# Rounding the gated activations of two chunks in one instruction, with a longer lag to the second product

## The chip, the cores and the metric

One core of one Trainium2 chip runs the kernel. The metric is the device time of one execution in microseconds; a figure for a kernel is the median of several executions.

## The reference, cut to what matters

Three steps run on 8192 tokens of 192 channels in float32: a causal depthwise convolution of seven softmaxed taps, and two feed-forward layers of width 2048, the first with `h * clip(h + 3, 0, 6) / 6` between its two products, the second with ELU.

```python
out = np.einsum('hk,bskhg->bshg', w, x_unf)      # seven taps, softmaxed, per head
...
h = x @ w_in;  g = h * np.clip(h + 3.0, 0.0, 6.0) / 6.0;  x = g @ w_out
...
h = x @ w_in;  g = np.where(h > 0.0, h, np.exp(np.minimum(h, 0.0)) - 1.0);  out = g @ w_out
```

## The kernel before, in words

**Blocks and chunks.** The tokens are cut into 16 blocks of 512 columns; the width of 2048 into 16 chunks of 128. The unit of the order is a chunk of one block of one layer: the list `slots` (L539 to 546) has 512 of them. The text counts layers as the code does: layer 0 (the clipped one) and layer 1 (ELU). Blocks 0 to 5 of layer 0 come first (blocks 0 and 1 interleaved, slots 0 to 31, then 32 to 95), then blocks of layer 1 and of layer 0 alternate, and the last six blocks of layer 1 follow each other.

**Products in two parts.** TensorE takes fp32r operands, so each operand is kept as a rounded part and a rest. `mm1` (L435) makes h of one chunk with five matmuls (four or five of half the contraction in the later stage), `mm2` (L479) adds the chunk into the output sums p with five: the rounded `gh` against three slices of weights, the rest `gl` against two. In the first stage (`stream(ALL, ...)`, slots 0 to `BOTH + LAG - 1`) each matmul uses all 128 rows. After it two streams, the lower and the upper 64 rows of the array, run side by side, the upper one eight matmuls behind; that stage is issued by hand in the order written (`manual_schedule`). A one-element memset of `relay` on POOL (L454) marks the end of each chunk's lower half of h.

**Between the products.** `first_done` (L680) is called when h of slot s is issued. `gate` (L460) makes g from h: one ScalarE activation (two in layer 1: Relu, then Exp in place) into a tile u, and one VectorE `scalar_tensor_tensor` from u and h into a tile g. `split_g` (L472) rounds g into `gh` on ScalarE (CAST) and takes `gl = g - gh` on VectorE; it is called for slot s-1 after the gate of s. h has three PSUM banks, so the first matmul of slot s+3 waits for the gate of slot s. `mm2` of slot s-LAG follows `mm1` of slot s; LAG is 4.

**The planner.** Everything else on VectorE and ScalarE is cut into steps (generators that yield) and put into `jobs` with a first slot a, a last slot e and a count n: decoding the float64 weights, the convolution of later blocks (`conv_main`, `conv_r`), the evaluation of a finished block (`upper_sum`) and the split of layer 0's result (`split_y`). `run_jobs` (L521) runs after each `first_done`; its function `wanted` decides:

```python
if s >= e() - (1 if e() <= BOTH else 2):
    return True
late = done * (e() - a) < n * (s - a + 1)
return late or s < BOTH + LAG and s >= a and debt[0] < 0 and debt[1] < 500
```

So in the later stage a job's steps are spread evenly over its slots, and what is left at the end is run at once. Of several wanted jobs the one with the earliest end goes first.

**Layer 0's result.** `upper_sum` (L367) adds the two halves of a finished block. The rest channels (64 of 192) are kept twice: `yr` of 128 rows is made with two ScalarE copies and one VectorE add; `split_y` (L416) rounds each half on ScalarE and subtracts each half on VectorE.

Of the kernel before, what the change touches and what calls it, by code (L numbers as in the profile page):

```python
# [8 lines left out]
F32 = mybir.dt.float32  # L9
F32R = mybir.dt.float32r  # L10
I32 = mybir.dt.int32
U32 = mybir.dt.uint32
AF = mybir.ActivationFunctionType
ALU = mybir.AluOpType
# [1 line left out]
PSUM = bass.MemoryType.PSUM  # L16

P = 128
LAG = 4
BEHIND = 8  # L20
RA = 6
STAG = 2
# [7 lines left out]
NB = 512  # L30
# [26 lines left out]
def conv_moe_moe2(ctx: ExitStack, tc: tile.TileContext, x, weight, w_in1, w_out1, w_in2, w_out2, out):  # L57
# [28 lines left out]
    LO, UP, ALL = slice(0, R), slice(R, P), slice(0, P)  # L86
    NBLK = NT // NB

    vec, act = Meter(nc.vector, 80), Meter(nc.scalar, 90)
# [3 lines left out]
    xin = ctx.enter_context(tc.tile_pool(name="xin", bufs=2))  # L93
    cv = ctx.enter_context(tc.tile_pool(name="cv", bufs=1))
    tmp = ctx.enter_context(tc.tile_pool(name="tmp", bufs=2))
    gp = ctx.enter_context(tc.tile_pool(name="gp", bufs=LAG + 1))
    yp = ctx.enter_context(tc.tile_pool(name="yp", bufs=RA - 1))
    op = ctx.enter_context(tc.tile_pool(name="op", bufs=3))
    ps_h = ctx.enter_context(tc.tile_pool(name="ps_h", bufs=3, space=PSUM))
# [9 lines left out]
    three = const.tile([P, 1], F32, name="three")  # L109
# [217 lines left out]
    def ring():  # L327


        A = op.tile([P, NB], F32R, name="opA", tag="opA")  # L330
        Bt = op.tile([P, NB], F32R, name="opB", tag="opB")
        lh = op.tile([P, NB], F32R, name="opC", tag="opC")
        hl = op.tile([P, NB], F32R, name="opD", tag="opD")
        return A, Bt, lh, hl
# [17 lines left out]

    spare = {}

    def lower_sum(l, b, lower):

        k = SIXTH if l == 0 else 1.0
        if l == 0:
            y0 = yp.tile([P, NB], F32, name="y0", tag="y0")
        else:  # L360
            y2 = stage.tile([P, 2 * NB], F32, name="y2", tag="raw")
            y0, spare[b] = y2[:, 0:NB], y2[:, NB:2 * NB]
        act.mul(y0, lower[0], k)
        s1 = tmp.tile([P, NB], F32, name="s1", tag="s1", bufs=1)
        act.mul(s1, lower[1], k)
        return y0, s1

    def upper_sum(l, b, upper, y0, s1):


        k = SIXTH if l == 0 else 1.0
        if upper is None:
            yield
        else:
            for i, y in enumerate((y0, s1)):
                vec.scalar_tensor_tensor(out=y, in0=upper[i], scalar=k, in1=y, op0=ALU.mult, op1=ALU.add)
                yield
        if l == 0:
            yr = yp.tile([P, NB], F32, name="yr", tag="yr")
        else:  # L380
            yr = spare.pop(b)
            out0 = store(b, 0, y0)
            next(out0)
        act.copy(yr[LO], s1[UP])
        if l == 0:
            act.copy(yr[UP], s1[LO])
        else:
            yield from out0
        yield
        h = ALL if l == 0 else LO  # L390
        vec.tensor_tensor(out=yr[h], in0=s1[h], in1=yr[h], op=ALU.add)
        yield
        if l == 1:
            yield from store(b, 1, yr)
        else:
            ys[b] = y0, yr

    def store(b, part, y):

        if part == 0:  # L400
            zs[b] = stage.tile([P, 2 * NB], F32, name="z", tag="raw")
        z = zs[b][:, part * NB:(part + 1) * NB]
        h = (ALL, LO)[part]
        vec.transpose(out=z[h], in_=y[h])
        yield
        for k in range(B):
            to = out[k * S + b * HB:k * S + (b + 1) * HB, part * P:part * P + h.stop].rearrange(
                "(j r) d -> r j d", r=SQ)
            for i in range(h.stop // SQ):
                queue = nc.scalar if b == NBLK - 1 and i % 2 else nc.sync  # L410
                queue.dma_start(to[:, :, i * SQ:(i + 1) * SQ],
                                z[i * SQ:(i + 1) * SQ, k * HB:(k + 1) * HB].rearrange("r (j c) -> r j c", c=SQ))
        yield
# [3 lines left out]
    def split_y(b):  # L417
        y0, yr = ys.pop(b)
        A, Bt, lh, hl = opnd[1, b] = ring()
        act.copy(A, y0)  # L420
        yield
        act.copy(hl[LO], yr[LO])
        vec.tensor_tensor(out=Bt, in0=y0, in1=A.bitcast(F32), op=ALU.subtract)
        yield
        act.copy(lh[UP], yr[UP])
        vec.tensor_tensor(out=lh[LO], in0=yr[LO], in1=hl[LO].bitcast(F32), op=ALU.subtract)
        yield
        vec.tensor_tensor(out=hl[UP], in0=yr[UP], in1=lh[UP].bitcast(F32), op=ALU.subtract)
        yield


    hs = {}
# [24 lines left out]
                tc.add_manual_dep(mm.ins, left.pop(s).ins.name, COMES_AFTER, reason="the lower half has left the bank")  # L457
            yield

    def gate(l, h):  # L460
        g = tmp.tile([P, NB], F32, name="g", tag="g")
        u = tmp.tile([P, NB], F32, name="u", tag="u")
        if l == 0:
            act.activation(u, h, AF.Relu, bias=three)
            vec.scalar_tensor_tensor(out=g, in0=u, scalar=6.0, in1=h, op0=ALU.min, op1=ALU.mult)
        else:
            act.activation(u, h, AF.Relu, scale=-1.0)
            act.activation(u, u, AF.Exp, scale=-1.0)
            vec.scalar_tensor_tensor(out=g, in0=u, scalar=-1.0, in1=h, op0=ALU.add, op1=ALU.max)
        return g  # L470

    def split_g(g):  # L472
        gh = gp.tile([P, NB], F32R, name="gh", tag="gh")
        act.copy(gh, g)
        gl = gp.tile([P, NB], F32R, name="gl", tag="gl")
        vec.tensor_tensor(out=gl, in0=g, in1=gh.bitcast(F32), op=ALU.subtract)
        return gh, gl

    acc = {}  # L479

# [17 lines left out]
    slots = [(0, 0, f) for f in range(STAG)]  # L498
# [7 lines left out]
    NS = len(slots)  # L506
# [12 lines left out]
    def job(gen, n, a, e):  # L519

        jobs.append([e if callable(e) else lambda: e, a, gen, n, 0])  # L521

    debt = [0, 0]

    def run_jobs(s, before):


        for i, (eng, w) in enumerate(zip((vec, act), before)):
            debt[i] = min(max(debt[i] - PACE, -PACE), -PACE // 2) + eng.work - w

        def wanted(jb):
            e, a, _, n, done = jb
            if s >= e() - (1 if e() <= BOTH else 2):
                return True
            late = done * (e() - a) < n * (s - a + 1)
            return late or s < BOTH + LAG and s >= a and debt[0] < 0 and debt[1] < 500

        while True:
            todo = [j for j in jobs if wanted(j)]  # L539
            if not todo:  # L540
                break
            jb = min(todo, key=lambda j: j[0]())
            w = vec.work, act.work
            if next(jb[2], jobs) is jobs:
                jobs.remove(jb)
            jb[4] += 1
            debt[0] += vec.work - w[0]
            debt[1] += act.work - w[1]
# [9 lines left out]
    def due(item):  # L558
        kind, l, a, e = item
        return at[l, 0, a] + (LAG if kind == "out" else 0)  # L560

# [65 lines left out]
    opnd[0, 0] = ring()  # L627
    weights = prepare()
    d0 = yp.tile([P, NB], F32, name="diag0", tag="y0")
    d1 = yp.tile([P, NB], F32, name="diag1", tag="yr")  # L630
    diag = [(d0, d1)[k // 4][:, k % 4 * P:(k % 4 + 1) * P] for k in range(K)]
    main = conv_main(0, taps_tensor)
    with tc.manual_schedule():
# [26 lines left out]
    for b in range(2, NBLK):  # L660
        e = at[0, b, 0] - 2
        if b <= RA:
            t = at[0, b - 1, 0]
        else:
            t = at[1, b - RA - 1, NF - 3]
            e = at[1, b - RA, NF - 3]
        job(feed(b), 1, t - 8, t - 7)
        job(whole(squares(b), conv(b)), 2 + CONV, t, e)
    for b in range(NBLK):
        e = at[1, b, 0]  # L670
        job(split_y(b), 4, e - 8, e - 2)

    gs = {}
    raw_g = {}

    def split(s):
        if s in raw_g:
            gs[s] = split_g(raw_g.pop(s))

    def first_done(s):  # L680
        w = vec.work, act.work
        raw_g[s] = gate(slots[s][0], hs.pop(s))
        split(s - 1)
        run_jobs(s, w)

    def second_done(s, half):
# [3 lines left out]
        if f == NF - 1:  # L690
            if half is not UP:
                sums[l, b] = lower_sum(l, b, acc.pop((l, b, False)))
            if half is not LO:
# [4 lines left out]
                else:  # L698
                    job(ev, 4 + 3 * l, min(s + LAG, NS - 1), min(s + LAG, NS - 1) + 4)

    sums = {}
    BOTH = at[0, 2, 0]

    def stream(half, slots1, behind):

        for s in slots1:
            if s < NS:
                yield from mm1(s, half)
            ends = s >= behind and half is UP and slots[s - LAG][2] == NF - 1
            if s < NS and half is not LO and not ends:  # L710
                first_done(s)
            if s >= behind:
                yield from mm2(s - LAG, half)
                second_done(s - LAG, half)
            if s < NS and ends:
                first_done(s)
            if s == NS - 1 and half is not LO:
                split(s)

    drain(stream(ALL, range(BOTH + LAG), LAG))  # L720
    with tc.manual_schedule():
        ends = {}
        n = {LO: 0, UP: BEHIND}
# [47 lines left out]
```

## Time and profile before

| what | value |
|---|---|
| median of three executions | 1184.96 us (1184.85 to 1185.17) |
| the profiled execution | 1185.06 us, of which the span is 1183.3 us |
| PE (matmuls) busy | 1165.6 us, 99% of the span |
| PEld (weight loads) busy | 989.6 us, 84% |
| DVE (VectorE) busy | 941.9 us, 80% |
| ACT (ScalarE) busy | 929.9 us, 79% |
| TensorE clock granted | 0.998 of full speed over the span |

Busy time is the union of an engine's instructions. Matmuls are pipelined and their ends are modelled, so two that follow each other overlap in the records; the time between starts tells the rate. The costliest lines are the second product (L493) and the first (L452); the chain that ended last lies on PE for 90% of the span, on DVE for 5% and on ACT for 3%.

### The profile page before, as it was taken

How to read it: one execution, taken by the hardware profiler on the slowest of the kernel's cores; microseconds unless marked ns; L12 is line 12 of the kernel's file. 1: busy time of each engine (PE TensorE's matmuls, PEld its weight loads, DVE VectorE, ACT ScalarE, POOL GpSimd, SP SyncE). 2: the span in 40 equal slices, each digit the busy share in tenths (PEclk: the TensorE clock that was granted, in tenths of full speed). 3: DMA queues.
4: the chain of work that ended last, by engine and by line, in shares of the span. 5: the costliest groups of instructions: out<-in, count | busy, mean ns of one | idle time of the engine just before them, and what ended most of it. 6: DMA issues, size and time to landing. Idle time of an engine off the chain costs nothing.

```text
span 1183.3 us, 25182 instructions
## 1 busy us (share of the span) xinstructions
PE 1165.6 (99%) x9496; PEld 989.6 (84%) x9496; DVE 941.9 (80%) x1607; ACT 929.9 (79%) x1683; POOL 44.2 (4%) x490
## 2 busy tenths in 40 slices
PE   8999999999999999999999999999999999999997
PEld 6778976788988889888898888988899888987776
DVE  8999899998878777787877878778787766777774
ACT  6777876888696877869788696877869678888885
POOL 0000000000000000000000000000000000000000
PEclk9999999999999999999999999999999999999999
DMA  6421111100101000010100101000000000000000
GB/s 169 109 70 32 33 51 36 41 2 6 23 1 28 1 17 13 1 28 1 28 2 6 24 1 29 1 16 13 2 15 2 14 1 6 10 15 15 15 14 16
DMA packets 108091, 26.81 MB, mean 23 GB/s; under 512 B 99648, under 2 KB 106816, under 8 KB 107968
## 3 DMA queue, kind: packets, MB, share of 16 engines
q1 hardware_dynamic: 106320, 24.99, 10.1%
q8 instruction: 74, 1.21, 0.4%
q14 instruction: 49, 0.40, 0.1%
q10 hardware_dynamic: 1648, 0.20, 0.1%
HBM read 18.87 MB, written 6.29 MB: 21 GB/s over the span
## 4 chain that ended last, share of the span: by engine, by line
PE 90%; DVE 5%; ACT 3%; issue 1%; ACTq 0%; DVEq 0%
PE p L493 45%; PE h L452 44%; ACT u L51 2%; DVE g L51 2%; DVE gl L51 1%; DVE acc L51 1%; PE psc L291 1%; ACT y L51 1%; DVE s L51 0%; DVE cw L51 0%; ACT gh L51 0%; DVE xw L51 0%; ACT opC L51 0%; ACT s L51 0%; PE psx L248 0%
## 5 line engine op out<-in xcount | busy, mean ns | idle before, releaser
L493 PE MATMUL p<-gh,wo 64*128 64x512 f32 (+1 forms) x2976 | 658.5, 393 | 0.8 <-ACT wo L51 0.5
L493 PE MATMUL p<-gl,wo 64*128 64x512 f32 (+1 forms) x1984 | 535.1, 391 | 0.0
L51 DVE SCALAR_TENSOR_TENSOR g<-u,h 128x512 f32<-128x512 f32 x512 | 349.7, 683 | 211.0 <-ACT u L51 207.6
L493 PEld LDWEIGHTS p<-gh,wo 64*128 64x128 f32 (+1 forms) x2976 | 466.6, 185 | 51.6 <-ACT wo L51 1.0
L51 DVE TENSOR_TENSOR gl<-g,gh 128x512 fp32r<-128x512 f32 x512 | 349.6, 683 | 0.6 <-ACT gh L51 0.4
L493 PEld LDWEIGHTS p<-gl,wo 64*128 64x128 f32 (+1 forms) x1984 | 316.4, 161 | 28.4 <-DVE gl L51 0.3
L51 ACT CAST gh<-g 128x512 fp32r<-128x512 f32 x512 | 311.6, 609 | 24.6 <-DVE g L51 24.1
L51 ACT ACTIVATE u<-h,three 128x512 f32<-128x512 f32 x256 | 175.9, 688 | 110.0 <-PE h L452 108.0
L452 PE MATMUL h<-opA,wi1h 64*128 64x512 f32 x512 | 200.8, 398 | 0.4
L452 PE MATMUL h<-opA,wi1l 64*128 64x512 f32 x512 | 200.4, 397 | 0.0
L452 PE MATMUL h<-opB,wi1h 64*128 64x512 f32 x512 | 197.0, 390 | 0.0
L452 PE MATMUL h<-opA,wi0h 64*128 64x512 f32 (+1 forms) x476 | 189.6, 401 | 4.3 <-DVE g L51 3.2
L51 ACT ACTIVATE u<-h 128x512 f32<-128x512 f32 x256 | 152.7, 596 | 48.0 <-PE h L452 45.8
L452 PE MATMUL h<-opA,wi0l 64*128 64x512 f32 (+1 forms) x476 | 188.7, 399 | 0.0
L452 PE MATMUL h<-opB,wi0h 64*128 64x512 f32 (+1 forms) x476 | 185.3, 391 | 0.0
L51 ACT ACTIVATE u<-u 128x512 f32<-128x512 f32 x256 | 161.9, 632 | 8.3
L452 PE MATMUL h<-opD,wi1r 64*128 64x512 f32 x384 | 149.4, 393 | 0.0
L452 PE MATMUL h<-opC,wi1r 64*128 64x512 f32 x384 | 148.5, 390 | 0.0
L452 PE MATMUL h<-opC,wi0r 64*128 64x512 f32 (+1 forms) x366 | 143.0, 392 | 0.4 <-ACT opC L51 0.4
L452 PE MATMUL h<-opD,wi0r 64*128 64x512 f32 (+1 forms) x366 | 143.4, 393 | 0.0
L452 PEld LDWEIGHTS h<-opA,wi0h 64*128 64x128 f32 (+1 forms) x476 | 87.6, 184 | 24.7 <-DVE g L51 12.5
L51 DVE SCALAR_TENSOR_TENSOR acc<-xT,taps,acc 128x256 f32<-128x256 f32 (+1 forms) x180 | 106.9, 599 | 0.1
(83 smaller groups left out, 1249.6 us busy)
## 6 DMA issues: line engine op xcount, KB each, us to landing
raw<-in_moe_w_out_dram SPq DMA_DIRECT2D x16, 384.0 KB, 3.2
out_dram<-z SPq DMA_DIRECT2D x186, 32.0 KB, 1.6
raw<-in_moe_w_in_dram SPq DMA_DIRECT2D x7, 512.0 KB, 3.8
x_sq<-in_x_dram SPq DMA_DIRECT2D x112, 32.0 KB, 2.2
raw<-in_moe_w_in_dram SPq DMA_DIRECT2D x8, 256.0 KB, 3.8
xr_sq<-in_x_dram SPq DMA_DIRECT2D x56, 32.0 KB, 2.1
x_sb<-in_x_dram SPq DMA_DIRECT2D x4, 128.0 KB, 3.0
raw<-in_moe_w_in_dram SPq DMA_DIRECT2D x4, 128.0 KB, 3.6
```

The lines of the kernel that those rows point to most:

```text
L51: return fn(*args, **kw)
L291: nc.tensor.matmul(ps[:, n * HB:(n + 1) * HB], diag[k], q[:, n, k:k + HB], start=k == 0, stop=k == K - 1)
L452: mm = nc.tensor.matmul(h, k, m[half], start=low and i == 0, stop=high and i == len(todo) - 1)
L493: nc.tensor.matmul(p[:n], k[:, :n], m[half], start=first and not end and k is not w0l, stop=last and end == 1)
```

## The change: two chunks per rounding, LAG 5, one copy of the rest

- u is gone: `gate` works in place in g. g is a pair tile of two chunks (`[128, 2, 512]`, two buffers), and so are `gh` and `gl` (three buffers in place of five single ones).
- `split_g` runs at even slots, for slots s-2 and s-1, with one CAST and one subtraction of 1024 columns. The last two slots are split singly.
- LAG is 5.
- In the later stage `wanted` lets spread jobs run at odd slots only, for two slots' worth of steps; the clause for the end stays as it was, at any slot.
- The rest of layer 0's result is kept once: an even block's in the lower 64 rows of a pair tile, an odd block's in the upper. `upper_sum` has one ScalarE copy in place of two; `split_y` has four ScalarE copies in place of three and two VectorE subtractions in place of three, the fourth copy reading what the second subtraction wrote.

```diff
-LAG = 4
+LAG = 5
...
-        act.copy(yr[LO], s1[UP])
-        if l == 0:
-            act.copy(yr[UP], s1[LO])
-        else:
+        act.copy(yr[h], s1[other])
+        if l == 1:
             yield from out0
         yield
-        h = ALL if l == 0 else LO
         vec.tensor_tensor(out=yr[h], in0=s1[h], in1=yr[h], op=ALU.add)
...
-        act.copy(hl[LO], yr[LO])
+        h, other = (UP, LO) if b % 2 else (LO, UP)
+        hi, lo = (lh, hl) if b % 2 else (hl, lh)
+        act.copy(hi[h], yr[h])
         vec.tensor_tensor(out=Bt, in0=y0, in1=A.bitcast(F32), op=ALU.subtract)
         yield
-        act.copy(lh[UP], yr[UP])
-        vec.tensor_tensor(out=lh[LO], in0=yr[LO], in1=hl[LO].bitcast(F32), op=ALU.subtract)
+        act.copy(lo[other], hi[h].bitcast(F32))
+        vec.tensor_tensor(out=lo[h], in0=yr[h], in1=hi[h].bitcast(F32), op=ALU.subtract)
         yield
-        vec.tensor_tensor(out=hl[UP], in0=yr[UP], in1=lh[UP].bitcast(F32), op=ALU.subtract)
+        act.copy(hi[other], lo[h].bitcast(F32))
...
+        g, gh, gl = (t[:, a:a + n] for t in pair)
         act.copy(gh, g)
-        gl = gp.tile([P, NB], F32R, name="gl", tag="gl")
         vec.tensor_tensor(out=gl, in0=g, in1=gh.bitcast(F32), op=ALU.subtract)
...
-            late = done * (e() - a) < n * (s - a + 1)
-            return late or s < BOTH + LAG and s >= a and debt[0] < 0 and debt[1] < 500
+            if s < BOTH + LAG:
+                return done * (e() - a) < n * (s - a + 1) or s >= a and debt[0] < 0 and debt[1] < 500
+            return s % 2 == 1 and done * (e() - a) < n * (s - a + 2)
...
-        raw_g[s] = gate(slots[s][0], hs.pop(s))
-        split(s - 1)
+        if s % 2 == 0:
+            pairs[s] = [tmp.tile([P, 2, NB], F32, name="g", tag="g")]
+        gate(slots[s][0], hs.pop(s), pairs[s - s % 2][0][:, s % 2])
+        if s == NS - 1:
+            split_g(s - 1, 1)
+        elif s % 2 == 0:
+            split_g(s - 2, 2)
```

## Rows read from the trace of the kernel before

**Rows 1.** The page, part 1: busy time, share of the span, instructions.
```profile
PE 1165.6 (99%) x9496; PEld 989.6 (84%) x9496; DVE 941.9 (80%) x1607; ACT 929.9 (79%) x1683; POOL 44.2 (4%) x490
```

**Rows 2.** Waits over the whole span: waiter <- releaser, us in total, times, longest.
```profile
PEld h L452 <- DVE g L51: 17.5, 42, 1.4
...
PE h L452 <- DVE g L51: 3.2, 5, 1.0
```

**Rows 3.** Timeline of POOL: one relay memset per chunk (start, us, instruction).
```profile
105.23 0.09 POOL L454 MEMSET relay<- 1x1 f32 x1 [102.18 <-PE h L452]
...
149.54 0.09 POOL L454 MEMSET relay<- 1x1 f32 x1 [2.24 <-PE h L452]
...
205.75 0.09 POOL L454 MEMSET relay<- 1x1 f32 x1 [2.01 <-PE h L452]
209.25 0.09 POOL L454 MEMSET relay<- 1x1 f32 x1 [3.41 <-PE h L452]
...
699.92 0.09 POOL L454 MEMSET relay<- 1x1 f32 x1 [2.00 <-PE h L452]
...
708.78 0.09 POOL L454 MEMSET relay<- 1x1 f32 x1 [2.00 <-PE h L452]
...
1167.38 0.09 POOL L454 MEMSET relay<- 1x1 f32 x1 [2.00 <-PE h L452]
```

**Rows 4.** Waits from 145 to 210 us.
```profile
PEld h L452 <- DVE g L51: 8.3, 11, 1.4
...
ACT opD L51 <- DVE opC L51: 3.1, 2, 1.6
```

**Rows 5.** Timeline of DVE, one chunk's worth in the dense stretch.
```profile
154.94 0.68 DVE L51 SCALAR_TENSOR_TENSOR g<-u,h 128x512 f32<-128x512 f32 x1
155.54 0.68 DVE L51 TENSOR_TENSOR gl<-g,gh 128x512 fp32r<-128x512 f32 x1
156.14 0.55 DVE L51 SCALAR_TENSOR_TENSOR xw<-xw,cw 128x384 int32<-128x384 int32 x1
156.61 1.14 DVE L51 SCALAR_TENSOR_TENSOR acc<-xT,taps,acc 128x256 f32<-128x256 f32 x2
157.67 0.68 DVE L51 SCALAR_TENSOR_TENSOR g<-u,h 128x512 f32<-128x512 f32 x1
```

**Rows 6.** Timeline of ACT at the end of one block's convolution.
```profile
165.95 0.41 ACT L51 CAST opD<-opC 64x256 fp32r<-64x256 f32 x1 [1.57 <-DVE opC L51]
...
166.84 0.69 ACT L51 ACTIVATE u<-h,three 128x512 f32<-128x512 f32 x1
```

**Rows 7.** By-form groups: busy us, mean ns | idle before.
```profile
L51 DVE TENSOR_TENSOR gl<-g,gh 128x512 fp32r<-128x512 f32 x512 | 349.6, 683 | 0.6 <-ACT gh L51 0.4
L51 ACT CAST gh<-g 128x512 fp32r<-128x512 f32 x512 | 311.6, 609 | 24.6 <-DVE g L51 24.1
...
L51 ACT COPY yr<-s 64x512 f32<-64x512 f32 x32 | 19.8, 620 | 2.5 <-DVE s L51 1.9
...
L51 DVE TENSOR_TENSOR opD<-yr,opC 64x512 fp32r<-64x512 f32 x16 | 11.0, 689 | 0.5
...
L51 DVE TENSOR_TENSOR wo<-xw,wo 128x256 fp32r<-128x256 f32 x16 | 6.6, 415 | 0.0
...
L51 ACT CAST wi0h<-xw 128x256 fp32r<-128x256 f32 x2 | 0.8, 406 | 0.7 <-DVE xw L51 0.7
```

**Rows 8.** Timelines of ACT, then of PEld, after a late block of layer 1.
```profile
1038.54 0.62 ACT L51 COPY y<-s 64x512 f32<-64x512 f32 x1 [1.45 <-DVE s L51]
...
1041.10 0.18 PEld L452 LDWEIGHTS h<-opA,wi1h 64*128 64x128 f32 x1 [0.50 <-DVE g L51]
```

**Rows 9.** Windows of 25 us: length, then busy us and instructions of each engine.
```profile
25.00:50.00 25.00, 24.52 (x105) 18.68 (x104) 24.49 (x48) 20.61 (x41) 0.00 (x0) 1.00 0.45 103
50.00:75.00 25.00, 24.41 (x101) 17.98 (x100) 24.91 (x51) 17.35 (x31) 0.00 (x0) 1.00 0.30 83
```

**Rows 10.** Timeline of PE in the last 20 us.
```profile
1171.11 0.72 PE L493 MATMUL p<-gh,wo 64*128 64x512 f32 x3 [0.24 <-ACT gh L51]
```

More of the change, by code (lines that the diff above doesn't have):

```diff
@@ L95, in conv_moe_moe2 @@
     tmp = ctx.enter_context(tc.tile_pool(name="tmp", bufs=2))
-    gp = ctx.enter_context(tc.tile_pool(name="gp", bufs=LAG + 1))
+    gp = ctx.enter_context(tc.tile_pool(name="gp", bufs=LAG // 2 + 1))
     yp = ctx.enter_context(tc.tile_pool(name="yp", bufs=RA - 1))
@@ L353, in conv_moe_moe2 @@
     spare = {}
+    rests = {}
     def lower_sum(l, b, lower):
@@ L377, in upper_sum @@
                 yield
+        h, other = (UP, LO) if l == 0 and b % 2 else (LO, UP)
         if l == 0:
-            yr = yp.tile([P, NB], F32, name="yr", tag="yr")
+            if b % 2 == 0:
+                rests[b // 2] = yp.tile([P, NB], F32, name="yr", tag="yr", bufs=RA // 2)
+            yr = rests[b // 2]
         else:
@@ L458, in mm1, with gate, split_g @@
             yield
-    def gate(l, h):
-        g = tmp.tile([P, NB], F32, name="g", tag="g")
-        u = tmp.tile([P, NB], F32, name="u", tag="u")
+    def gate(l, h, g):
         if l == 0:
-            act.activation(u, h, AF.Relu, bias=three)
-            vec.scalar_tensor_tensor(out=g, in0=u, scalar=6.0, in1=h, op0=ALU.min, op1=ALU.mult)
-        else:
[L467 to L473, printed above, removed]
+            act.activation(g, h, AF.Relu, bias=three)
+            vec.scalar_tensor_tensor(out=g, in0=g, scalar=6.0, in1=h, op0=ALU.min, op1=ALU.mult)
+        else:
+            act.activation(g, h, AF.Relu, scale=-1.0)
+            act.activation(g, g, AF.Exp, scale=-1.0)
+            vec.scalar_tensor_tensor(out=g, in0=g, scalar=-1.0, in1=h, op0=ALU.add, op1=ALU.max)
+    pairs = {}
+    def split_g(s, n):
+        a = s % 2
+        if s - a not in pairs:
+            return
+        pair = pairs[s - a]
+        if len(pair) == 1:
+            pair += [gp.tile([P, 2, NB], F32R, name=k, tag=k) for k in ("gh", "gl")]
+        g, gh, gl = (t[:, a:a + n] for t in pair)
         act.copy(gh, g)
-        gl = gp.tile([P, NB], F32R, name="gl", tag="gl")
         vec.tensor_tensor(out=gl, in0=g, in1=gh.bitcast(F32), op=ALU.subtract)
-        return gh, gl
+        for k in range(n):
+            gs[s + k] = gh[:, k], gl[:, k]
     acc = {}
@@ L629, in conv_moe_moe2 @@
     d0 = yp.tile([P, NB], F32, name="diag0", tag="y0")
-    d1 = yp.tile([P, NB], F32, name="diag1", tag="yr")
+    d1 = yp.tile([P, NB], F32, name="diag1", tag="yr", bufs=RA // 2)
     diag = [(d0, d1)[k // 4][:, k % 4 * P:(k % 4 + 1) * P] for k in range(K)]
@@ L673, in conv_moe_moe2 @@
     gs = {}
[L674 to L678, printed above, removed]
     def first_done(s):
         w = vec.work, act.work
-        raw_g[s] = gate(slots[s][0], hs.pop(s))
-        split(s - 1)
+        if s % 2 == 0:
[5 more added lines that the diff above has]
+            split_g(s - 2, 2)
         run_jobs(s, w)
@@ L717, in stream @@
             if s == NS - 1 and half is not LO:
-                split(s)
+                split_g(s, 1)
     drain(stream(ALL, range(BOTH + LAG), LAG))
```

## The prediction, made before the change was run

> **What bounds the kernel now.** The page's busy times come first: PE is busy for 1165.6 of 1183.3 us, VectorE and ScalarE for about four fifths [rows 1]. A busy PE need not be at its pace, so next I read the marks that POOL leaves once per chunk. In a quiet stretch four chunks take 708.78 - 699.92 = 8.86 us, 2.215 each, which for nine and a half matmul pairs is 0.233 us a pair [rows 3]. From the first mark to the last lie 475 chunks in 1062.15 us; at the quiet pace they would take 475 x 2.215 = 1052.1. So the two-stream stage loses 10.0 us in all, and no change on VectorE or ScalarE can win more there: the matmuls stay.
>
> Where do the 10.0 us lie? The waits name one cause almost alone: TensorE's weight load and matmul of h wait for the gate g on VectorE [rows 2], because h has three banks. Between the marks at 149.54 and 209.25 there are 24 chunks, which should take 53.2 us and take 59.7: 6.5 us are lost in this dense stretch, where the second layer's weights are decoded beside two convolutions, and its waits have the same name [rows 4]. The other 3.5 us are spread over 400 chunks, up to 0.5 us at a time after the ends of blocks [rows 8]. Ahead of the stage PE is idle for 0.48 + 0.59 us between 25 and 75 us [rows 9], and near the end 0.24 us for a rounding that comes late [rows 10].
>
> The dense stretch shows two mechanisms. First, VectorE is simply full: from one gate to the next it spends 157.67 - 154.94 = 2.73 us without a gap, where a chunk should take 2.215 [rows 5]. Second, ScalarE blocks itself: at the end of a convolution block its copy waits 1.57 us for VectorE, and the activation u of the next chunk stands behind it [rows 6]. The 3.1 us of such waits [rows 4] are followed by a chunk of 209.25 - 205.75 = 3.50 us [rows 3], about 1.2 more than usual, and they occur twice.
>
> **The change, part by part.**
>
> *One rounding and one subtraction for two chunks.* No instruction of 1024 columns is in the trace. The subtraction takes 683 ns for 512 columns and 415 for 256 [rows 7], so 1.05 ns a column, and 1024 would be about 1219: 147 ns less than two. But in a full queue two instructions start 0.60 us apart [rows 5], not 0.683; a merged one, overlapping its successor by the same 0.083, holds the queue for 1.136 in place of 1.20, a saving of 0.064. The value I take is 0.064, as time on VectorE counts only where the queue is full. The bounds are 0 (the overlap of the halves was all there was to save) and 0.147. Over the 12 pairs of the dense stretch that is 0.8 us (0 to 1.8); elsewhere VectorE has room and the saving is worth nothing by itself. The rounding on ScalarE (609 and 406 ns [rows 7]) saves at most 2 x 609 - 1015 = 203 ns a pair, hidden under PE everywhere but behind a block's end.
>
> [...]
>
> *Jobs at odd slots only.* An even slot carries a gate and the pair's subtraction, an odd slot a gate and two slots' worth of steps. The total is the same, so a full VectorE stays full; but the target counts one slot ahead, so a convolution's steps spread over 15 slots in place of 14. Two convolutions of some 7 us on VectorE (an estimate: six pairs of a main and a rest step at 1.14 us [rows 5]) thin out by 1/15, about 0.5 us each: 1.0 us (0 to 1.0). More important is the end: by `wanted`, only the last step was still left at the end clause (the other three used to run there with it), so the copy no longer stands in ScalarE's queue ahead of the subtraction that it waits for. That takes away the two blocked activations: 2 x 1.2 = 2.3 us (0 to 2.4).
>
> *What lumps cost.* After a block's end three or more steps of `upper_sum` now fall into one odd slot. In layer 0 the add on VectorE then stands right behind the sum it needs, with a ScalarE copy of 620 ns [rows 7] between: VectorE waits some 0.6 us. Where it is full that is lost: two block ends in the stretch, 1.2 us (0 to 1.3). Elsewhere it is covered by the slack of the three banks. How large that is shows a late block: a wait of 1.45 us on ScalarE cost PE 0.50 [rows 8], so about 1 us was free, and a wait of 0.6 hides under it. In `split_y` the new fourth copy waits in ScalarE's queue for the subtraction in the same slot; behind it stands the next chunk's u, for at most a gate and a subtraction (683 and 689 ns [rows 7]) less the copy in between (620): 0.75 us, under the same slack. If that cover is gone, each costs a few tenths, some 16 times. One subtraction less per block is worth nothing where VectorE has room. The output DMAs of a layer 1 block are issued a slot later on SP's queue; nobody waits for them before the last block, whose steps run at once as before.
>
> *u in place of g, and the pair buffers.* The activation that opens a pair must wait until the pair two before has been subtracted, about two slots earlier. It is late only if VectorE is already a chunk behind, and then its gate would wait too: nothing (up to 1 us in the stretch).
>
> *LAG 5.* The extra lag covers what pairing takes: the first of a pair is rounded one slot later than before, and used one slot later. One more slot runs its first product at full width, five matmuls in place of 4.5 pairs: 0.1 us more. The first layer's output weights are due one slot later, which may take back part of the 1.07 us of idle PE before 75 us [rows 9]: 0.2 us (from -1 to 1, as that stage's order is the scheduler's and may come out otherwise). At the end the last rounding has one more chunk of matmuls before it: the 0.24 us [rows 10] go.
>
> *After late blocks of layer 1* the sum and its copy now move to the slot behind, so that the copy no longer holds up ScalarE right after a gate that is itself late. Five such ends cost up to 0.5 us each [rows 8]; I take 0.2 from each, 1.0 us (from -0.5 to 2).
>
> **The sum.** Dense stretch: 0.8 + 1.0 + 2.3 - 1.2 = 2.9. Late blocks 1.0, start 0.2, end 0.2, wider slot -0.1. Together 4.2 us. The profiled execution took 1185.06 us (1183.3 and 1.8 around the span); 1185.06 - 4.2 = 1180.9, and the median of the runs lies 0.1 below it: **1180.8 us**.
>
> **The rivals.**
>
> *The queue stays full* (chance 0.20). VectorE in the dense stretch has nothing to give: 2.73 us a chunk for a need of 2.215 [rows 5], and the waits of the block ends eat the 0.064 a pair. Then only the ends win, and time is about 1185.0 - 1.5 = 1183.5: no change. For it speaks that 0.8 us of true saving is small against 6.5 lost; against it, that part of the 6.5 is ScalarE's own blocking [rows 6].
>
> *All waits go* (0.15). If spreading by pairs also lets the banks carry each peak, most of the 10.0 + 1.07 + 0.24 us come back: 1185 - 11.2 = 1173.8. Against it: two chunks at 2.73 are 5.46 us, and the merged pair takes off only 0.064.
>
> *Lumps become a wait of their own* (0.07), slower: at each of the 16 layer 0 block ends VectorE waits 0.62 us for the copy, and the gate of the next chunk comes after more than the free 1 us of slack. The point is an odd slot whose steps and wait exceed that; in layer 1's slots, with two activations per chunk, it is nearest. Price 16 x 0.62 = 9.9 us, and no gain in the dense stretch but 1.3 at late blocks, start and end: 1185.0 + 9.9 - 1.3 = 1193.6. Against it: a measured wait of 1.45 cost only 0.50 [rows 8].
>
> *The pairs are not joined* (0.03): if the builder cuts a 1024-column instruction in two, the 0.8 falls away and the rest stays: 1181.6.
>
> **How the numbers follow.** The forecast has 0.55 and by its bounds spans about 1178 to 1183. A measurement of this kernel tells a change from none at about 0.2%, 2.4 us, so faster means below 1182.6. Faster: 0.52 of the forecast's 0.55, 0.15 and 0.03, together 0.70; within 0.2%: 0.03 and 0.20, 0.23; slower 0.07. The range leaves out the slower rival and the far half of the one in which all waits go, and takes in the full queue with a little for the start: 1176.0 to 1184.8.
>
> **What would show it.** In the profile after: subtractions and casts of 128x1024, some 255 of each, near 1.2 and 1.0 us; marks in the dense stretch about 3 us closer together; no long ScalarE wait for `opC` there; the gate waits of PEld down to about half of 17.5 us; a new VectorE wait of yr for ScalarE at layer 0 block ends; the quiet pace still 2.215. I am wrong if the stretch is as long as before, if PE waits for `gl` or for the copies after block ends, or if the start shifts by more than a microsecond.

## The result, and the profile after

The changed kernel takes 1196.32 us (median of five, 1195.69 to 1196.73) against 1184.96 before: a ratio of 1.0095, 95% interval 1.0085 to 1.0106. It is 11.4 us slower; the forecast was 1180.8 and the range ended at 1184.8. The profiled execution took 1195.69 us with a span of 1194.0, 10.7 more than the span before.

The page of the changed kernel, part 1, stands against [rows 1]:

```profile
PE 1166.8 (98%) x9492; PEld 976.5 (82%) x9492; DVE 933.4 (78%) x1336; ACT 905.5 (76%) x1428; POOL 44.3 (4%) x489
```

VectorE and ScalarE do what was meant: 271 and 255 instructions fewer, 8.5 and 24.4 us less busy. PE is busy about as long as before (1.2 us more) and idle for longer (27.2 us of the span in place of 17.7). Its by-form groups and a full stretch of its VectorE queue answer to [rows 7] and [rows 5]:

```profile
L51 DVE TENSOR_TENSOR gl<-g,gh 128x1024 fp32r<-128x1024 f32 x255 | 311.9, 1223 | 45.7 <-ACT gh L51 43.9 <-PE h L456 1.0
L51 ACT CAST gh<-g 128x1024 fp32r<-128x1024 f32 x255 | 264.8, 1038 | 4.2 <-DVE g L51 4.2
```

```profile
222.59 1.22 DVE L51 TENSOR_TENSOR gl<-g,gh 128x1024 fp32r<-128x1024 f32 x1
223.72 0.69 DVE L51 SCALAR_TENSOR_TENSOR xw<-xw,cw 128x512 int32<-128x512 int32 x1
```

The pairs are joined, and one holds the queue for 1.13 us. The quiet pace is the old one: between these marks of the changed kernel lie four chunks in 8.86 us, as in [rows 3].

```profile
107.04 0.09 POOL L458 MEMSET relay<- 1x1 f32 x1 [103.99 <-PE h L456]
...
337.04 0.09 POOL L458 MEMSET relay<- 1x1 f32 x1 [2.25 <-PE h L456]
340.08 0.09 POOL L458 MEMSET relay<- 1x1 f32 x1 [2.95 <-PE h L456]
...
708.71 0.09 POOL L458 MEMSET relay<- 1x1 f32 x1 [2.00 <-PE h L456]
717.57 0.09 POOL L458 MEMSET relay<- 1x1 f32 x1 [2.00 <-PE h L456]
...
1177.04 0.09 POOL L458 MEMSET relay<- 1x1 f32 x1 [2.00 <-PE h L456]
```

In the quiet stretch a mark comes 2.09 us after the one before it for an odd chunk and 2.34 for an even one; losses at a single end are counted against these. The mark at 340.08 (an odd chunk) comes 3.04 us after the one before it, 0.95 too late. Such a step stands at nine of the ten layer 0 block ends behind chunk 113; the last one has none. The waits of the whole span, against [rows 2], have the old name at 1.7 times the size on PEld and four times on PE, and new rows beside it:

```profile
PEld h L456 <- DVE g L51: 29.7, 48, 1.7
...
ACT g L51 <- DVE gl L51: 25.6, 29, 2.1
...
ACT yr L51 <- DVE s L51: 17.4, 14, 2.2
PE h L456 <- DVE g L51: 12.9, 19, 1.3
DVE yr L51 <- ACT yr L51: 9.6, 14, 0.7
```

The marks show where the time lies. The table gives, for stretches of chunks (one mark per chunk, the last for chunk 511), the time between the first and the last mark less 2.215 us a chunk: what is lost there. It is worked out from POOL's timeline of each kernel; the runs below are named in the next section.

| us lost in chunks | 37 to 81 (dense) | 81 to 113 | 113 to 417 | 417 to 511 | in all |
|---|---|---|---|---|---|
| before | 6.5 | 0.1 | 1.8 | 1.7 | 10.1 |
| after | 7.3 | 3.1 | 9.8 | -0.1 | 20.1 |
| e1, jobs at every slot | 9.8 | 1.6 | 10.8 | 6.0 | 28.2 |
| e3, single instructions | 7.6 | 3.3 | 11.9 | -0.1 | 22.7 |
| e7, both sums first | 5.9 | 3.5 | 1.1 | -0.1 | 10.4 |
| e9, rest once alone | 6.7 | 0.0 | 1.1 | 1.8 | 9.5 |
| e6, lag 5 and rest once | 6.8 | 0.3 | 3.8 | 3.9 | 14.9 |
| e10, before with a late sum | 9.4 | 3.7 | 14.6 | 2.5 | 30.1 |
| e13, e7 with single chunks in 82 to 113 | 5.9 | 0.7 | 1.2 | -0.1 | 7.6 |

So the 10.7 us are: +0.8 in the dense stretch, +3.0 in chunks 81 to 113, +8.0 in 113 to 417, -1.8 in the late blocks, and +0.7 outside the marks (start and end). The largest part is the layer 0 block ends. This is one of them, in the changed kernel's timelines of ACT, DVE and PEld:

```profile
333.24 0.63 ACT L51 ACTIVATE g<-g 128x512 f32<-128x512 f32 x1
335.23 0.62 ACT L51 COPY yr<-s 64x512 f32<-64x512 f32 x1 [1.35 <-DVE s L51]
335.87 0.41 ACT L51 CAST opD<-acc 64x256 fp32r<-64x256 f32 x1
336.29 0.40 ACT L51 CAST opC<-acc 64x256 fp32r<-64x256 f32 x1
336.72 0.60 ACT L51 ACTIVATE g<-h 128x512 f32<-128x512 f32 x1
```

```profile
334.51 0.68 DVE L51 SCALAR_TENSOR_TENSOR s<-p,s 128x512 f32<-128x512 f32 x1
335.88 0.68 DVE L51 TENSOR_TENSOR yr<-s,yr 64x512 f32<-64x512 f32 x1 [0.69 <-ACT yr L51]
338.01 0.69 DVE L51 SCALAR_TENSOR_TENSOR g<-g,h 128x512 f32<-128x512 f32 x1 [1.45 <-ACT g L51]
```

```profile
338.76 0.18 PEld L456 LDWEIGHTS h<-opA,wi1h 64*128 64x128 f32 x1 [1.12 <-DVE g L51]
```

From the end of one chunk's activations (333.87) to the start of the next chunk's (336.72) ScalarE spends 2.85 us: 1.35 waiting for the sum s, then the copy, then two casts of the convolution. VectorE waits 0.69 us for the copy, but behind the add it has nothing to do for another 1.45 us. The gate ends at 338.70, and PE's weight load has been waiting for it for 1.12 us.

The last layer 0 end has the same order of instructions, but no convolution is left to do there. Its rows on ACT:

```profile
980.46 0.63 ACT L51 ACTIVATE g<-g 128x512 f32<-128x512 f32 x1
982.45 0.62 ACT L51 COPY yr<-s 64x512 f32<-64x512 f32 x1 [1.36 <-DVE s L51]
983.10 0.60 ACT L51 ACTIVATE g<-h 128x512 f32<-128x512 f32 x1
```

The copy waits as long, but with no cast behind it the next activation comes after 2.01 us and not after 2.85, and the mark behind it (986.66) comes at the usual 2.09 us. So the wait costs what it does together with the casts that stand behind it on ScalarE. At the end shown first, 2.85 us between the activations cost 0.95, so some 1.9 us were free; at the last one 2.01 cost nothing, where ScalarE also runs 0.3 us further ahead of the marks.

### The profile page after: what moved, and what is told of

The parts are those of the page before. It is cut to its first block, busy times and chain, and to the rows that moved or that the text cites. A ratio compares the mean times of both kernels' runs of the same rounds, so it can differ in the third digit from the quotient of the medians.

```text
span 1194.0 us, 24038 instructions
## 1 busy us (share of the span) xinstructions
PE 1166.8 (98%) x9492; PEld 976.5 (82%) x9492; DVE 933.4 (78%) x1336; ACT 905.5 (76%) x1428; POOL 44.3 (4%) x489
## 4 chain that ended last, share of the span: by engine, by line
PE 86%; DVE 8%; ACT 4%; issue 1%; ACTq 0%; DVEq 0%
PE p L503 44%; PE h L456 42%; DVE g L51 2%; ACT g L51 2%; DVE gl L51 2%; DVE acc L51 2%; ACT gh L51 1%; DVE cw L51 1%; DVE xw L51 0%; ACT opC L51 0%; DVE y L51 0%; ACT opD L51 0%; DVE s L51 0%; DVE wo L51 0%; ACT yr L51 0%
## 5 line engine op out<-in xcount | busy, mean ns | idle before, releaser
L503 PE MATMUL p<-gh,wo 64*128 64x512 f32 (+1 forms) x2976 | 564.0, 393 | 0.6 <-ACT wo L51 0.5
L51 DVE SCALAR_TENSOR_TENSOR g<-g,h 128x512 f32<-128x512 f32 x512 | 350.1, 684 | 158.2 <-ACT g L51 154.7
L503 PE MATMUL p<-gl,wo 64*128 64x512 f32 (+2 forms) x1984 | 441.1, 391 | 0.3 <-DVE gl L51 0.3
L51 DVE TENSOR_TENSOR gl<-g,gh 128x1024 fp32r<-128x1024 f32 (+1 forms) x257 | 313.2, 1219 | 45.8 <-ACT gh L51 43.9
L503 PEld LDWEIGHTS p<-gl,wo 64*128 64x128 f32 (+2 forms) x1984 | 260.9, 161 | 35.2 <-DVE gl L51 0.7
L51 ACT ACTIVATE g<-h,three 128x512 f32<-128x512 f32 x256 | 175.9, 688 | 125.9 <-PE h L456 100.2
L51 ACT CAST gh<-g 128x1024 fp32r<-128x1024 f32 (+1 forms) x257 | 266.0, 1035 | 4.4 <-DVE g L51 4.4
L51 ACT ACTIVATE g<-h 128x512 f32<-128x512 f32 x256 | 152.6, 596 | 52.0 <-PE h L456 42.1
L51 ACT ACTIVATE g<-g 128x512 f32<-128x512 f32 x256 | 161.9, 633 | 8.1
L456 PEld LDWEIGHTS h<-opA,wi1h 64*128 64x128 f32 x512 | 94.2, 184 | 22.5 <-DVE g L51 14.9
```

The lines of the kernel that those rows point to most:

```text
L51: return fn(*args, **kw)
L456: mm = nc.tensor.matmul(h, k, m[half], start=low and i == 0, stop=high and i == len(todo) - 1)
L503: nc.tensor.matmul(p[:n], k[:, :n], m[half], start=first and not end and k is not w0l, stop=last and end == 1)
```

## The experiments

Twelve kernels ran. The changed kernel with u in a tile of its own was not among them. The runs of the kernel before beside them had medians of 1184.90 to 1185.24 us.

**e1: jobs at every slot.**

```diff
-            return s % 2 == 1 and done * (e() - a) < n * (s - a + 2)
+            return done * (e() - a) < n * (s - a + 1)
```

> The changed kernel, but spread jobs may run at every slot again, with the target of before. Theory A (jobs lumped into odd slots: behind a layer 0 block's end ScalarE's copy waits for the sum on VectorE in the same slot, and the next chunk's activation stands behind it): the nine steps of 0.75 to 0.95 us that the marks show every 32 chunks go, and part of what the stretch up to chunk 113 lost: 1181 to 1186 us. Theory B (instructions of 1024 columns hold up the queues or come late): no better than 1193. Theory C (g in place: the activation waits for the subtraction two pairs before, 25.6 us in the waits view): no better than 1193.

Measured: 1204.43 us (ratio 1.0164, 1.0148 to 1.0179). My first theory, that the odd-slot rule does the damage, fell as it stood: without the rule the changed kernel is 8 us slower still. (Theories B and C both allowed this time; e3 is the test of B.) The layer 0 ends behind chunk 113 do lose less, 0.4 to 0.6 us in place of 0.95, but every layer 1 end there loses 0.64 in place of 0.16, and each of the five late ones 1.2 to 1.4 in place of nothing. The ScalarE and PEld timelines of e1 behind a layer 1 end show the wait:

```profile
371.25 0.62 ACT L51 COPY y<-s 64x512 f32<-64x512 f32 x1 [2.39 <-DVE s L51]
```

```profile
373.35 0.18 PEld L456 LDWEIGHTS h<-opA,wi0h 64*128 64x128 f32 x1 [0.82 <-DVE g L51]
```

By the order of the code a job's step at an even slot stands on VectorE behind the subtraction of a pair, 1.22 us long; the copy waited 2.39 us in ScalarE's queue. Beside pairs, the odd-slot rule won more than it cost here (8 us).

**e2: only upper_sum at every slot.**

```diff
+            if jb[2] in sum_jobs:
+                return done * (e() - a) < n * (s - a + 1)
             return s % 2 == 1 and done * (e() - a) < n * (s - a + 2)
...
+                    sum_jobs.append(ev)
```

> The changed kernel, but the jobs of upper_sum alone may run at every slot; the convolution and split_y stay at odd slots. Theory A, if it is the block's end itself: nine steps of about 0.85 us go, 1196.3 - 7.7 = 1188.6; if it is the convolution's casts lumped beside it, less than 3 us go. Theories B and C: unchanged within 1 us.

Measured: 1205.37 us (1.0172, 1.0155 to 1.0189), none of the three. Layer 0 ends still lose 0.9 to 1.1 us, and layer 1 ends now 0.65 in place of 0.16. At the layer 0 end shown above the copy waits 0.73 us in place of 1.35 and 2.22 us lie between the activations in place of 2.85; the chunk behind it loses 0.31 in place of 0.95, less by the same 0.6. But the chunk after that now loses 0.56 as well. These are e2's rows on VectorE, and PEld's wait:

```profile
337.23 1.22 DVE L51 TENSOR_TENSOR gl<-g,gh 128x1024 fp32r<-128x1024 f32 x1 [0.26 <-ACT gh L51]
338.38 0.68 DVE L51 TENSOR_TENSOR yr<-s,yr 64x512 f32<-64x512 f32 x1
338.98 0.67 DVE L51 SCALAR_TENSOR_TENSOR g<-g,h 128x512 f32<-128x512 f32 x1
```

```profile
339.70 0.18 PEld L456 LDWEIGHTS h<-opA,wi1h 64*128 64x128 f32 x1 [0.75 <-DVE g L51]
```

The add now stands behind the pair's subtraction and holds up the next gate.

**e3: single instructions.**

```diff
-        act.copy(gh, g)
-        vec.tensor_tensor(out=gl, in0=g, in1=gh.bitcast(F32), op=ALU.subtract)
         for k in range(n):
+            act.copy(gh[:, k], g[:, k])
+            vec.tensor_tensor(out=gl[:, k], in0=g[:, k], in1=gh[:, k].bitcast(F32), op=ALU.subtract)
```

> The changed kernel, but each pair's rounding and subtraction are issued as two instructions of 512 columns, at the same place. Theory A: unchanged or up to 3 us longer (the 0.064 us of queue per pair, where VectorE or ScalarE is late). Theory B: most of the 11 us come back, about 1187.

Measured: 1198.10 us (1.0110, 1.0095 to 1.0125), 1.8 over the changed kernel, as theory A had it. Joining the instructions helps a little; the longer instructions are not what costs.

**e5: the kernel before with jobs at odd slots.**

```diff
-            return late or s < BOTH + LAG and s >= a and debt[0] < 0 and debt[1] < 500
+            if s < BOTH + LAG:
+                return late or s >= a and debt[0] < 0 and debt[1] < 500
+            return s % 2 == 1 and done * (e() - a) < n * (s - a + 2)
```

> The kernel before, with the one edit that in the later stage spread jobs run at odd slots only, for two slots' worth of steps. Theory A: slower, by the block ends after layer 0 and the lumps in the dense stretch, 1188 to 1196 (with a lag of 4 a block's end falls on an odd slot, so its first two steps still run there, and the loss may be smaller than with a lag of 5). Theories B and C: within 1 us of 1185.

Measured: 1208.01 us (1.0194, 1.0179 to 1.0210), above what any of the theories gave. The same rule that saves the paired kernel 8 us costs the unpaired one 23. Its layer 0 ends behind chunk 113 lose 1.6 to 1.7 us each (the last 1.1): the sum and both copies of the rest run in one slot, and the copies (1.25 us) wait for the sum, 1.46 us at the same place in ScalarE's timeline.

**e6 and e9: the lag and the single copy of the rest, in the kernel before.** e9 takes the change's `upper_sum`, `split_y` and `rests` alone; e6 has the lag of 5 as well:

```diff
-LAG = 4
+LAG = 5
```

> The kernel before with two parts of the change alone: the lag of 5 (six single buffers for gh and gl) and the rest of layer 0's result kept once. Chunks are rounded singly, jobs run at every slot, u has its own tile. Theory D (the damage is done by grouping two chunks' roundings at one slot, beside a planner that was balanced for one rounding per slot): 1183 to 1187 us. Rival E (a block's end moved by the lag to an even slot, or the fourth copy of split_y in ScalarE's queue): most of the 11 us stay, 1191 to 1197.

> The kernel before with the rest of layer 0's result kept once, and nothing else. Both theories D and A2: within 1.5 us of 1185, as one ScalarE copy less at a block's end is worth little where PE is busy. Rival E, as far as the fourth copy goes: 1188 or more.

Measured: e9 1184.59 us (0.9995, 0.9986 to 1.0005), no change; e6 1190.03 us (1.0041, 1.0026 to 1.0056), between the two expectations. The lag alone costs 5.4 us. Both kernels have the same wait behind a late layer 1 block; these are its rows on ACT and on PEld, for e9 and then for e6:

```profile
1038.22 0.62 ACT L51 COPY y<-s 64x512 f32<-64x512 f32 x1 [1.45 <-DVE s L51]
```

```profile
1040.77 0.18 PEld L456 LDWEIGHTS h<-opA,wi1h 64*128 64x128 f32 x1 [0.50 <-DVE g L51]
```

```profile
1043.70 0.62 ACT L51 COPY y<-s 64x512 f32<-64x512 f32 x1 [1.45 <-DVE s L51]
```

```profile
1046.25 0.18 PEld L456 LDWEIGHTS h<-opA,wi1h 64*128 64x128 f32 x1 [0.97 <-DVE g L51]
```

The same 1.45 us on ScalarE cost PE 0.50 with a lag of 4 and 0.97 with 5. The lag moves a block's end from an odd to an even slot. The lower stream's first product has five matmuls for even chunks and four for odd ones (`mm1`), so the slack behind a slot would depend on its parity; two matmul pairs of 0.233 us are the 0.47 between the rows. That this parity is the cause is argued from the code and not tested by itself.

**e7: both sums of a layer 0 block ahead of the gate.**

```diff
                 next(ev)
+                if l == 0:
+                    next(ev)
```

> The changed kernel, but for layer 0 both sums of a finished block (y and s) are issued on VectorE together, ahead of the gate, so that the copy in the next odd slot finds s ready. Theory A2 (the price of a layer 0 block's end is ScalarE's 1.35 us wait for s with the next activation behind it): most of the eleven steps of 0.8 to 1.3 us behind layer 0 blocks go, 1187 to 1190. If the gate that now stands behind one more sum is what PE waits for, nothing is won: 1195 to 1198.

Measured: 1186.64 us (1.0012, 1.0002 to 1.0021), just under theory A2's range: 9.7 us of the 11.4 come back with one more step at the block's end. The layer 0 ends from chunk 129 on lose nothing now. The same place on ACT in e7:

```profile
332.20 0.64 ACT L51 ACTIVATE g<-g 128x512 f32<-128x512 f32 x1
332.86 0.62 ACT L51 COPY yr<-s 64x512 f32<-64x512 f32 x1
333.50 0.41 ACT L51 CAST opD<-acc 64x256 fp32r<-64x256 f32 x1
333.92 0.40 ACT L51 CAST opC<-acc 64x256 fp32r<-64x256 f32 x1
334.35 0.60 ACT L51 ACTIVATE g<-h 128x512 f32<-128x512 f32 x1
```

The copy starts at once. The same three instructions stand between the activations, but they take 1.5 us and not 2.85, and that fits into the 1.9 us or so that were free there in the changed kernel.

**e8: the parity turned.** Pairs are slots 1 and 2, 3 and 4, rounded at odd slots; jobs run at even slots, where the blocks end.

```diff
-            return s % 2 == 1 and done * (e() - a) < n * (s - a + 2)
+            return s % 2 == 0 and done * (e() - a) < n * (s - a + 2)
...
-        a = s % 2
+        a = (s + 1) % 2
```

> The changed kernel with the parity turned: pairs are slots 1 and 2, 3 and 4 and so on, rounded at odd slots, and spread jobs run at even slots; a block's end (slot 16k+4) then has the job slot and not the rounding slot. Theory A2: the sum s and its copy run in the block's end slot itself, before the pair's rounding, as in the kernel before: 1183 to 1189. If grouping as such costs the time wherever the end lies (theory D): 1193 to 1199.

Measured: 1216.84 us (1.0268, 1.0250 to 1.0286), the slowest of all and far above both expectations. Its rows on ACT and PEld at the same block end:

```profile
337.10 0.62 ACT L51 COPY yr<-s 64x512 f32<-64x512 f32 x1 [1.36 <-DVE s L51]
337.73 0.62 ACT L51 CAST opA<-acc 128x512 fp32r<-128x512 f32 x1
...
339.10 0.60 ACT L51 ACTIVATE g<-h 128x512 f32<-128x512 f32 x1
```

```profile
341.13 0.18 PEld L456 LDWEIGHTS h<-opA,wi1h 64*128 64x128 f32 x1 [2.03 <-DVE g L51]
```

The sum did move into the end's slot, but its copy with it, so the wait is the same 1.36 us, and one more cast stands behind it (three casts in all). Moving the sum won nothing here, as its copy still shares the slot with it.

**e10: the suspected cause in the kernel before.** All that is left of a layer 0 sum runs in the slot behind the block's end: the second sum, both copies of the rest and the add.

```diff
-                    job(ev, 4 + 3 * l, min(s + LAG, NS - 1), min(s + LAG, NS - 1) + 4)
+                    if l == 0:
+                        job(ev, 4, s + LAG + 1, s + LAG + 3)
+                    else:
+                        job(ev, 4 + 3 * l, min(s + LAG, NS - 1), min(s + LAG, NS - 1) + 4)
```

> The kernel before, where after a layer 0 block the second sum, its two copies and the add all run in the one slot behind the block's end (before: the sum in the end's slot, the copies one slot later, the add two later). Theory A2: this alone makes the kernel before slower at each of the twelve layer 0 ends behind slot 47 by 0.7 to 1.5 us (two copies of 0.62 stand in ScalarE's queue here, one in the changed kernel): 1193 to 1200 us. If the price belongs to the pairs, within 2 us of 1185.

Measured: 1205.14 us (1.0167, 1.0153 to 1.0181), above the range I gave: 20 us with no pair, no lag and no odd rule. Its rows on ACT and PEld:

```profile
336.27 1.25 ACT L51 COPY yr<-s 64x512 f32<-64x512 f32 x2 [1.44 <-DVE s L51]
...
338.08 0.59 ACT L51 ACTIVATE u<-h 128x512 f32<-128x512 f32 x1
```

```profile
340.11 0.18 PEld L452 LDWEIGHTS h<-opA,wi1h 64*128 64x128 f32 x1 [1.48 <-DVE g L51]
```

Its ends behind chunk 113 lose 1.5 to 1.6 us each, the last one, with no convolution beside it, 0.8; the dense stretch loses 2.9 more than before. This is more than the changed kernel has in that slot: two copies (1.25 us) in place of one, so its 20 us are no measure of the changed kernel's price.

**e11 and e12: e7 with the add one slot behind its copy; and, on top, the second layer's weights from slot 38 on.**

```diff
-                    job(ev, 4 + 3 * l, min(s + LAG, NS - 1), min(s + LAG, NS - 1) + 4)
+                    job(ev, (1, 7)[l], min(s + LAG, NS - 1), min(s + LAG, NS - 1) + 4)
...
-W2 = (44, 120)
+W2 = (38, 120)
```

> The changed kernel with both layer 0 sums ahead of the gate, and the add of the rest one slot behind its copy (the copy alone in the odd slot). The wait of VectorE for the copy, 0.7 to 0.9 us at each layer 0 end, should go; it counts where VectorE is full (ends near slots 52, 68, 84 and 100): 1186.6 - 2.5 = 1184. If VectorE's wait was covered there too: 1186.6.

> The same, with the second layer's weights decoded from slot 38 on in place of slot 44 (to 120 as before). If the stretch from slot 49 to 113 is bound by VectorE's total, its load falls by about one step in twelve: another 1.5 to 2 us, 1182. If it is bound by lumps and not by the total: no change.

Measured: 1189.29 us (1.0034, 1.0022 to 1.0047) and 1189.76 (1.0038, 1.0025 to 1.0052). Both of e11's expectations failed. Of VectorE's waits for the copy (9.6 us in the changed kernel) e7's timelines show two, 0.92 and 0.80 us, and none at the end shown above, so there was little to win. e11 takes 2.7 us more than e7, and by the marks the second chunk behind the layer 0 ends from chunk 129 on loses 0.2 to 0.45 us where e7 loses nothing. That the add, now in the slot of the pair's subtraction, holds up a gate there as in e2 is an inference; no row shows it. e12 differs from e11 by 0.5 us, the "no change" of its second expectation: by the marks earlier weights only move the loss from chunks 81 to 113 (3.8 to 1.4 us) to chunks 37 to 81 (5.9 to 8.3).

**e13: e7, with slots 82 to 113 as before** (single roundings, jobs at every slot).

```diff
+            if s in SINGLE:
+                return done * (e() - a) < n * (s - a + 1)
...
+        elif s in SINGLE:
+            if s > SINGLE[0]:
+                split_g(s - 1, 1)
+            else:
+                split_g(s - 2, 2)
...
+SINGLE = range(82, 114)
```

> The changed kernel with both layer 0 sums ahead of the gate, and in slots 82 to 113 rounded singly with jobs at every slot, as in the kernel before. If grouping by pairs and odd slots is what costs the stretch from chunk 81 to 113 its 3.5 us (0.1 before), those come back: 1186.6 - 3.3 = 1183.3, under the kernel before. If the cost there is the layer 0 ends themselves or the lag of 5: within 1 us of 1186.6.

Measured: 1183.70 us (0.9989, 0.9980 to 0.9998), 1.2 us under the kernel before beside it (1184.90), as expected if grouping is what costs. The rows of PE's wait between 218 and 292 us, for the changed kernel and then for e13:

```profile
PEld h L456 <- DVE g L51: 4.4, 7, 1.5
PE h L456 <- DVE g L51: 2.0, 4, 1.1
```

```profile
PEld h L457 <- DVE g L52: 1.3, 3, 0.9
...
PE h L457 <- DVE g L52: 0.4, 1, 0.4
```

In this stretch, where the second layer's weights are still being decoded, grouping by pairs and odd slots costs some 2.8 us (3.5 in e7, 0.7 here); which of its jobs does it was not taken apart.

## Why the prediction was wrong

**What lumps cost: the step that failed.** It said that behind a layer 0 end VectorE waits some 0.6 us for the copy, and that this hides under about 1 us of slack. That wait exists (0.69 us in the timeline above) and does hide: behind the add VectorE is idle for another 1.45 us. The step looked at the wrong queue. In the same odd slot the copy itself waits 1.35 us on ScalarE for the sum, the convolution's casts follow it, and the next chunk's activation comes 2.85 us after the last one ended. Some 0.95 us of that is paid at each of nine ends, 8.5 us in all, where the prediction put nothing. The row that prices the wait was in hand: 1.45 us on ScalarE, with a copy behind it, cost PE 0.50 [rows 8]; here two casts (0.85 us) stand behind the copy as well, and without them, at the last end, the same wait costs nothing. e7 takes the wait away and wins 9.7 us; e10 puts it, with a second copy, into the kernel before and loses 20.

**The rival on the other side** named the place, the layer 0 ends, and its 1193.6 was near; but it gave VectorE's wait as the mechanism and had a chance of 0.07, so that its price was near (9.9 us) is luck. The three steps that `wanted` gathers into one slot were read from the code; whom they wait for, on each queue in order, was not followed.

**LAG 5** was priced at 0.1 us. In the unpaired kernel it costs 5.4 (e6 against e9); that this comes from moving every block's end to a slot with less slack is argued above, not shown. In e7 little of it is left by the marks (no loss at the late ends, 0.16 us at the other layer 1 ends); the layer 1 sums and copies there run at the odd slot behind.

**Jobs at odd slots.** Between 145 and 210 us the end clause went as said: the waits of `opD` for `opC` [rows 4] are gone there (over the whole span they grew, from 3.5 to 8.1 us). But in the changed kernel this row stands in their place:

```profile
ACT opD L51 <- DVE acc L51: 5.6, 2, 3.0
```

The copies no longer wait for the subtraction; lumped with the last taps, they wait for those. So the stretch loses 0.8 us more than before where I had forecast a gain of 2.9. With the sums in order (e7) its gain is 0.6 us.

**Behind the dense stretch** the prediction let nothing be lost, as "elsewhere VectorE has room". Its stretch ended at chunk 80, but weights are decoded for longer: in chunks 81 to 113 the changed kernel lost 3.0 us more than the kernel before, and e13 gets 2.8 back by undoing the grouping there. What in the grouping costs it is open.

**Right by mechanism:** the pair holds VectorE for 1.13 us (forecast 1.136). The worth of joining has the size of the forecast but not its place: e3 puts it at 1.8 us in all, and by the marks only 0.3 us of it lies in the dense stretch, where 0.8 was forecast; most lies at the layer 0 ends (1.12 us lost at each in e3, 0.95 with the pairs joined), where it was put at nothing. The late blocks won 1.8 us where 1.0 was forecast, with the sum and its copy in the slot behind. The rest kept once is worth nothing measurable (e9). The quiet pace stayed.

**The start and the end** lost time where 0.4 was to be won: together they cost 0.7 us. The windows of the changed kernel that answer to [rows 9] show PE idle for 1.70 us in place of 1.07:

```profile
25.00:50.00 25.00, 24.11 (x102) 18.15 (x101) 24.46 (x42) 20.31 (x35) 0.00 (x0) 1.00 0.45 103
50.00:75.00 25.00, 24.19 (x101) 17.71 (x100) 24.34 (x46) 15.96 (x26) 0.00 (x0) 1.00 0.30 82
```

The wait of 0.24 us near the end [rows 10] did not go either; PE now waits there for `gl`, which the prediction named as a sign of being wrong:

```profile
1180.25 0.49 PE L503 MATMUL p<-gl,wo 64*128 64x512 f32 x2 [0.29 <-DVE gl L51]
```

Why the start loses was not tested, nor was the pair tile in place of u: the new ScalarE wait for the subtraction (25.6 us in the waits) is nearly as long in e7 (25.0), which recovers nearly all, so it costs at most little.

## What to carry to other kernels

When work is regrouped in time, follow every instruction of the group on its own queue. Here a ScalarE copy of 0.62 us that came to share a slot with the sum it waits for held up two casts and the next activation behind it; the price was not the copy's time but 0.95 us, the queue's whole delay of 2.85 us (the wait of 1.35, the copy, the casts) less some 1.9 that were free. Idle time on a queue off the critical path was free here only up to such a slack, so measure the slack at the very place and in the very kernel: the same wait of 1.45 us cost 0.50 us in e9 and 0.97 in e6. A part that cost 23 us alone (e5) saved 8 beside another part (e1), so undo parts from both kernels before blaming one.

## What the runs showed that was not expected

The slack behind a wait is not a constant of the kernel: the same 1.45 us of ScalarE cost 0.50 or 0.97 us of TensorE time in two kernels that differ only in the lag (e9 and e6). And the block end that costs nothing, the last of layer 0, has the same wait (1.36 us) as the end shown of the nine that cost 0.95 us each (1.35). The joined instructions follow their width closely: 1223 ns for 1024 columns of subtraction where the line through 415 and 683 ns gives 1219, and 1038 ns for the rounding where 406 and 609 ns give 1015.
